# Means of k and v copied side by side and transposed in six full-height blocks, with loads and first folds re-placed

## The chip, the cores and the metric

The kernel runs on one core of one Trainium2 chip. The metric is the device time of one execution in microseconds (us), taken from the chip. Executions of one kernel mostly agree within about half a per cent here, so every comparison rests on several of them, taken in turns with the kernel before on the same chip. Traces have their own clock that starts with the first instruction; the span in a trace is 1 to 3 us shorter than the measured time.

## The reference, cut to what matters

Eight batches of eight heads, 576 tokens, head size 64, 32 memory slots. Each batch is an attention through the 32 slots, and its output feeds a bilinear feed-forward layer that all batches share:

```python
a   = softmax(phi, axis=2)                      # over the 32 slots
k_m = einsum('bhsm,bhsd->bhmd', a, k)           # means of k: per head 32 x 64
v_m = einsum('bhsm,bhsd->bhmd', a, v)           # means of v
attn = softmax(q @ k_m.T / 8)
x   = (attn @ v_m) laid out as tokens x 512
out = ((x @ w_a) * (x @ w_b)) @ w_out           # 512 -> 1536 -> 512
```

The kernel never forms `attn @ v_m`. It multiplies the means of v into w_a and w_b once per batch (a "fold"), and multiplies the weights of attention by that.

## The kernel before

The work of a batch is cut into named units: `exp` (exponential of phi, on ScalarE), `kv` (sums of k and v, on TensorE), `km` (division, giving the means `kvm`, on VectorE), `kvt` (transposes of the means), `qt` (32x32-block transposes of q, on VectorE), `sc` (scores), `e`, `den`, `nr` (softmax), `v0` to `v2` (folds; `x..` copies them out of PSUM). While TensorE does the big products of batch b (`pa`, `pb`, and the down products `po`), the units of batch b+1, and with a prime those of b+2, are dealt out over its 24 slots in a list. The part that the change replaces:

```python
def kv_transpose():
    kvm = t["kvm"]
    t["kvT"] = mid.tile([P, 6, P], F16, name="kvT")
    pT = banks.tile([P, 6, P], F16, name="pT")
    for g in range(2):
        for dh in range(2):
            for z in range(4):
                nc.tensor.transpose(out=pT[32 * z:32 * z + 32, 2 * g + dh, :],
                                    in_=kvm[:, g, 0, 32 * dh:32 * dh + 32],
                                    identity=ident, tile_position=(0, 32 * z))
    # ... and 8 more for the means of v: 24 transposes of 128 x 32 in all
    nc.vector.tensor_copy(out=t["kvT"], in_=pT)
```

Loads are issued by GpSimd; k, v and q become 16 bits wide on the way. phi and q have two buffers each, k and v share two:

```python
def load(b):
    load_phi(b); load_k(b); load_v(b); load_q(b)
# ...
for b in range(2, B):
    if b + 2 < B:
        load(b + 2)                  # at the start of each period
```

Batches 0 and 1 go through separate, denser lists, because the weights and the first inputs are still arriving. Batch 1's chain is filled up with early down products, the "fillers" ("y4" is four of them). A slot of the first folds is four `pa` or `pb` matmuls, 0.49 us; the prediction calls it a half-step.

The softmax here doesn't subtract the row's maximum and nothing guards it: scores larger than these inputs give would overflow.

## Time and profile before

| | before |
|---|---|
| time, median of 3 | 256.01 us (255.79 to 256.13) |
| TensorE (PE) busy | 242.8 us, 95% of the span |
| VectorE, ScalarE, GpSimd busy | 62%, 61%, 14% |
| DMA | full up to 82 us, then in bursts |
| six blocks of 24 small transposes | 0.55 us of TensorE each |

Matmuls are pipelined and their ends are modelled, so busy time says little about how much TensorE can still give. What counts is when one group starts after the one before it. In the views TensorE is PE (its weight loads PEld), VectorE DVE, ScalarE ACT and GpSimd POOL. The prediction shows the lines and how to read them.

### The profile page before, as it was taken

Reading aid. Unit: us, or ns where it says so; the run is one execution under the profiler, and the core shown is the slowest. Engines: PE = TensorE matmul, PEld = TensorE weight load, DVE = VectorE, ACT = ScalarE, POOL = GpSimd, SP = SyncE. Lnnn points to the kernel's source line nnn. Section 1 sums busy time; section 2 is a strip of 40 time slices with the busy share of each in tenths; the row PEclk is TensorE's granted clock in tenths of the full one; section 3 lists DMA queues with packets and bytes.
Section 4 is the critical chain, followed back from the end, with each engine's and each line's share of the span. In section 5 each row is a group of like instructions: output and inputs, shape, how many; then the busy total and the mean of one; then the engine's idle time right before and its main releaser. Section 6 shows DMA issues by size and latency. Waiting matters only on the chain.

```text
span 254.5 us, 7157 instructions
## 1 busy us (share of the span) xinstructions
PE 242.8 (95%) x2887; PEld 140.1 (55%) x2887; DVE 157.8 (62%) x349; ACT 155.7 (61%) x379; POOL 35.4 (14%) x54
## 2 busy tenths in 40 slices
PE   8789599999999999999999999999999999999993
PEld 3455274456554555556565556655665555666642
DVE  6347686367967856875985568746983567445400
ACT  3147472588479479758855777578856667555421
POOL 8733234300300310310121000000000000000000
PEclk9999999999999999999999999999999999999999
DMA  6999999999999696498359521112112112113233
GB/s 143 195 198 206 216 245 207 253 228 272 250 243 208 144 225 135 135 171 153 86 131 222 128 62 44 44 41 44 41 40 49 43 41 45 41 41 70 58 82 82
DMA packets 26033, 33.49 MB, mean 132 GB/s; under 512 B 1936, under 2 KB 20624, under 8 KB 26000
## 3 DMA queue, kind: packets, MB, share of 16 engines
q0 software_dynamic: 19552, 23.01, 50.0%
q1 hardware_dynamic: 6288, 9.90, 15.5%
q8 instruction: 22, 0.36, 0.5%
q10 hardware_dynamic: 160, 0.13, 0.2%
q14 instruction: 11, 0.09, 0.1%
HBM read 42.47 MB, written 9.44 MB: 204 GB/s over the span
## 4 chain that ended last, share of the span: by engine, by line
PE 80%; DMA 11%; DVE 3%; ACT 2%; issue 2%; POOL 1%; ACTq 0%; DVEq 0%; POOLq 0%
PE po L383 34%; PE pa L469 18%; PE pb L479 16%; DMA wb_sb<-in_moe_w_b_dram 6%; PE pva L330 5%; DMA kv_sb<-in_v_dram 4%; PE pkv L206 2%; PE pD L310 1%; PE pscore L288 1%; DVE qT L197 1%; DVE ht L482 1%; PE pk L253 1%; PE pT L232 1%; ACT a_sb L472 1%; POOL q_sb L89 1%
## 5 line engine op out<-in xcount | busy, mean ns | idle before, releaser
L482 DVE TENSOR_TENSOR ht<-a_sb,pb 128x288 f16<-128x288 f16 x192 | 84.1, 447 | 59.2 <-ACT a_sb L472 51.7
L383 PE MATMUL po<-wo_sb,ht 128*128 128x512 f16 x420 | 118.7, 379 | 0.0
L472 ACT CAST a_sb<-pa 128x288 f16<-128x288 f32 x192 | 75.4, 404 | 42.3 <-PE pa L469 36.9
L469 PE MATMUL pa<-A,vab 128*128 128x288 f16 x384 | 76.7, 287 | 0.9 <-DVE A L320 0.7
L479 PE MATMUL pb<-A,vab 128*128 128x288 f16 x384 | 76.1, 286 | 0.2
L469 PEld LDWEIGHTS <-vab 128*128 128x128 f16 x384 | 34.1, 98 | 40.0 <-issue 8.2
L383 PEld LDWEIGHTS <-ht 128*128 128x128 f16 x420 | 40.3, 98 | 19.2 <-issue 0.9
L479 PEld LDWEIGHTS <-vab 128*128 128x128 f16 x384 | 37.1, 98 | 11.7 <-ACT vab L342 1.1
L342 ACT CAST vab<-pva 128x512 f16<-128x512 f32 (+1 forms) x52 | 28.8, 557 | 14.9 <-PE pva L330 14.8
L342 DVE CAST vab<-pva 128x512 f16<-128x512 f32 (+1 forms) x52 | 33.4, 645 | 6.1 <-PE pva L330 5.6
L388 ACT ACTIVATE o_sb<-po 128x512 f32<-128x512 f32 x35 | 21.1, 602 | 11.0 <-PE po L383 9.9
L197 DVE STREAM_TRANSPOSE qT<-q_sb 128x576 f16<-128x576 f16 x32 | 24.2, 764 | 0.0
L301 ACT ACTIVATE E<-pscore 128x288 f16<-128x288 f32 x32 | 11.5, 419 | 13.1 <-PE pscore L288 13.1
L311 ACT ACTIVATE L<-pD 128x288 f32<-128x288 f32 x32 | 11.4, 409 | 8.3 <-PE pD L310 7.9
L145 PE MATMUL pw<-warm 128*128 128x256 f16 (+1 forms) x59 | 11.5, 340 | 1.3 <-DVE warm L114 1.3
L77 POOL DMA_DIRECT2D phi_sb<-in_phi_dram x7 | 5.3, 756 | 52.7 <-ACT a_sb L472 27.2
L188 ACT ACTIVATE exp_sb<-phi_sb 128x576 f16<-128x576 f32 x16 | 11.0, 698 | 2.5 <-DMA phi_sb<-in_phi_dram 2.5
L330 PEld LDWEIGHTS <-kvT 64*32 64x32 f16 x416 | 4.5, 89 | 14.1 <-issue 11.6
L320 DVE TENSOR_TENSOR A<-E,R 128x576 f16<-128x576 f16 (+1 forms) x17 | 7.5, 441 | 7.2 <-ACT R L319 6.2
L330 PE MATMUL pva<-wb_sb,kvT 64*32 64x512 f16 (+1 forms) x208 | 10.1, 362 | 1.9 <-DMA wb_sb<-in_moe_w_b_dram 1.9
L319 ACT ACTIVATE R<-L 128x576 f16<-128x576 f32 (+1 forms) x17 | 11.1, 664 | 0.1
L330 PE MATMUL pva<-wa_sb,kvT 64*32 64x512 f16 (+1 forms) x208 | 10.3, 370 | 0.7 <-DMA wa_sb<-in_moe_w_a_dram 0.7
(43 smaller groups left out, 107.2 us busy)
## 6 DMA issues: line engine op xcount, KB each, us to landing
out_dram<-o_sb SPq DMA_DIRECT2D x70, 128.0 KB, 2.4
kv_sb<-in_v_dram POOLq DMA_DIRECT2D x7, 576.0 KB, 10.5
phi_sb<-in_phi_dram POOLq DMA_DIRECT2D x7, 576.0 KB, 9.8
kv_sb<-in_k_dram POOLq DMA_DIRECT2D x7, 576.0 KB, 10.6
q_sb<-in_q_dram POOLq DMA_DIRECT2D x6, 576.0 KB, 11.2
wo_sb<-in_moe_w_out_dram POOLq DMA_DIRECT2D x3, 512.0 KB, 16.6
q_sb<-in_q_dram POOLq DMA_DIRECT2D x4, 288.0 KB, 12.8
wa_sb<-in_moe_w_a_dram POOLq DMA_DIRECT2D x2, 512.0 KB, 15.1
```

What stands on the lines that cost most here:

```text
L145: nc.tensor.matmul(pw[:, :cols], warm[:, :P], warm[:, :cols], start=True, stop=True)
L197: nc.vector.transpose(out=t["qT"][:, hp, :], in_=qs[b][:, hp, :])
L301: nc.scalar.activation(out=Ev[:, g, :, z, :], in_=pss, func=AF.Exp, scale=1.0 / (8.0 * CS))
L311: nc.scalar.activation(out=t["L", g][:, sl], in_=pD, func=AF.Ln)
L330: nc.tensor.matmul(t["pva", lo, z][g][0][32 * j:32 * j + 32, 0:hi - lo], t["kvT"][64 * r:64 * r + 64, 4 + g, M * j:M * j + M], w_sbs[z][64 ...
L342: engine_copy(out=vabs[b][z][:, g, lo:hi], in_=pva[:, 0:hi - lo])
L383: nc.tensor.matmul(po, hts[pair][:, i, P * c:P * (c + 1)], wo_sb[:, i, :], start=(i == 0), stop=(i == NFF - 1))
L388: nc.scalar.mul(out=o_sb, in_=po, mul=1.0 / (CS * CS))
L469: nc.tensor.matmul(pa, vab[0][:, g, fs], A[:, g, HALF * hf:HALF * (hf + 1)], start=(g == 0), stop=(g == 1))
L472: nc.scalar.copy(out=a_sb, in_=pa)
L479: nc.tensor.matmul(pb, vab[1][:, g, fs], A[:, g, HALF * hf:HALF * (hf + 1)], start=(g == 0), stop=(g == 1))
L482: nc.vector.tensor_tensor(out=ht[:, i, t0:t0 + HALF], in0=a_sbs[hf - hfs[0]], in1=pb, op=ALU.mult)
```

## The change

Its intent: TensorE is the bound, and 24 small transposes in another tiling mode (128*32 in the views, against 128*128) cost it more than six full-height ones. So GpSimd, which has little to do, first copies the means so that each block of 128 columns lies side by side, in the repeated order in which the small transposes placed it. Because GpSimd also issues the loads, those get places of their own ("L"). And the first folds, which had waited for weights, move later, with some filler re-ordered. Shortened:

```diff
+        def repeat():
+            t["rep"] = mid.tile([P, 2, 3, P], F16, name="rep")
+            k, v = (t["kvm"][:, :, x].rearrange("p g (e d) -> p g e d", e=2 - x) for x in range(2))
+            for g in range(2):
+                nc.gpsimd.tensor_copy(out=t["rep"][:, g, 0:2].rearrange("p e (z d) -> p e z d", z=4),
+                                      in_=k[:, g].unsqueeze(2).to_broadcast([P, 2, 4, 32]))
+            nc.gpsimd.tensor_copy(out=t["rep"][:, :, 2:3]...,  in_=v...to_broadcast([P, 2, 2, D]))
         def kv_transpose():
-            # 24 transposes of 128 x 32 at tile_position (0, 32 z)
+            for g in range(2):
+                for x in range(3):
+                    nc.tensor.transpose(out=pT[:, (2 * g + x, 4 + g)[x == 2], :], in_=t["rep"][:, g, x], identity=ident)
 ...
-    ups(steps(0, 4, 12), slots(0, "- v2a+x2a - v2b+x2b"))
-    chain(1, "exp0 exp1 y6 ks0 y4 kt0 qt0 qt1 y2 ks1 y4 kt1 s0 e0 qt2 qt3 y8 den0 s1 e1 nr0 y4 den1 nr1 y3 vs0 y1 vs1 y2 vt0 y1 vt1 y1 "
+    ups(steps(0, 4, 12), slots(0, "- - - - v2a+x2a - v2b+x2b"))
+    chain(1, "exp0 exp1 y9 ks0 y3 kt0 qt0 qt1 y1 ks1 y3 kt1 s0 e0 qt2 qt3 y6 den0 y2 s1 e1 nr0 y4 den1 y2 vs0 vs1 y1 vt0 vt1 nr1 y1 "
 ...   # batch 1's ups re-ordered likewise; in the list of batch 2 "... nr0+L exp0' ..." (load of batch 5)
-    every = ("- sc+e0 ... v2+kv'+x2a km'+x2b qt3' - kvt' -")
+    every = ("- sc+e0 ... v2+kv'+x2a km'+x2b rp' qt3' kvt' L")
     for b in range(2, B):
-        if b + 2 < B:
-            load(b + 2)
+        if b == 2:
+            load(4)
```

More of the change, by code (lines that the diff above doesn't have):

```diff
@@ L223, in take_kv @@
                 banks.free(bank)
+        def repeat():
[4 more added lines that the diff above has]
+                                      in_=k[:, g].unsqueeze(2).to_broadcast([P, 2, 4, 32]))
+            nc.gpsimd.tensor_copy(out=t["rep"][:, :, 2:3].rearrange("p g e (z d) -> p (g e) z d", z=2),
+                                  in_=v.rearrange("p g e d -> p (g e) d").unsqueeze(2).to_broadcast([P, 2, 2, D]))
         def kv_transpose():
-            kvm = t["kvm"]
             t["kvT"] = mid.tile([P, 6, P], F16, name="kvT")
@@ L229, in kv_transpose @@
             for g in range(2):
-                for dh in range(2):
-                    for z in range(4):
-                        nc.tensor.transpose(out=pT[32 * z:32 * z + 32, 2 * g + dh, :],
-                                            in_=kvm[:, g, 0, 32 * dh:32 * dh + 32],
-                                            identity=ident, tile_position=(0, 32 * z))
-            for g in range(2):
-                for z in range(4):
-                    nc.tensor.transpose(out=pT[32 * z:32 * z + 32, 4 + g, :],
-                                        in_=kvm[:, g, 1, 32 * (z % 2):32 * (z % 2) + 32],
-                                        identity=ident, tile_position=(0, 32 * z))
+                for x in range(3):
+                    nc.tensor.transpose(out=pT[:, (2 * g + x, 4 + g)[x == 2], :], in_=t["rep"][:, g, x], identity=ident)
             nc.vector.tensor_copy(out=t["kvT"], in_=pT)
@@ L372, in units @@
         u["km"] = one(take_kv)
+        u["rp"] = one(repeat)
         u["kvt"] = one(kv_transpose)
@@ L519, in unit @@
                 return lambda: work.pull(-work.done % NFF)
+            if n == "L":
+                return lambda: load(b + 2) if b + 2 < B else None
             if n[0] == "y":
@@ L549 @@
     load(2)
-    ups(steps(0, 4, 12), slots(0, "- v2a+x2a - v2b+x2b"))
-    chain(1, "exp0 exp1 y6 ks0 y4 kt0 qt0 qt1 y2 ks1 y4 kt1 s0 e0 qt2 qt3 y8 den0 s1 e1 nr0 y4 den1 nr1 y3 vs0 y1 vs1 y2 vt0 y1 vt1 y1 "
+    ups(steps(0, 4, 12), slots(0, "- - - - v2a+x2a - v2b+x2b"))
+    chain(1, "exp0 exp1 y9 ks0 y3 kt0 qt0 qt1 y1 ks1 y3 kt1 s0 e0 qt2 qt3 y6 den0 y2 s1 e1 nr0 y4 den1 y2 vs0 vs1 y1 vt0 vt1 nr1 y1 "
              "hv0a hx0a y2 hv0b hx0b y2")
     load(3)
-    ups(steps(1, 0, 4), slots(1, "- hv1a+hx1a hv1b+hx1b - v1a+x1a v1b+x1b y2 y2"))
+    ups(steps(1, 0, 4), slots(1, "y1 hv1a+hx1a hv1b+hx1b y1 v1a+x1a v1b+x1b y3 y3"))
     work.plan(S + HALF, 8)
     work.rate = 0
-    ups(half_steps(1, 0, 4), slots(1, "v2a+x2a v2b+x2b exp0'+y2 exp1'+y2 qt0' qt1'+y2 kv'+km' y2+qt2'"))
+    ups(half_steps(1, 0, 4), slots(1, "v2a+x2a+v2b+x2b y9 - exp0' exp1'+qt0' kv'+km' rp'+qt1' qt2'"))
     work.plan(S + HALF, 10)
-    ups(half_steps(1, 1, 4), slots(2, "qt3 kvt - sc+e0 e1 den0 v0+x0a den1+x0b nr0 nr1 v1+x1a x1b"))
-    second = ("v2_+x2a_ exp0+x2b_ exp1+qt0 kv+km qt1 kvt+qt2 qt3 - sc+e0 e1 v0+x0a x0b+den0 den1 v1+x1a x1b+nr0 exp0' nr1 exp1'+qt0' v2+x2a x2b "
-              "kv' km'+qt1' kvt'+qt2' qt3'")
-    every = ("- sc+e0 - e1 v0+x0a x0b den0 den1 exp0' qt0' v1+x1a x1b exp1' nr0 qt1' nr1 qt2' v2+kv'+x2a km'+x2b qt3' - kvt' -")
+    ups(half_steps(1, 1, 4), slots(2, "kvt qt3 - sc+e0 e1 den0 den1 v0+x0a nr0+x0b nr1 v1+x1a x1b"))
+    second = ("v2_+x2a_ exp0+x2b_ exp1+qt0 kv+km rp+qt1 qt2 kvt+qt3 - sc+e0 e1 v0+x0a x0b+den0 den1 v1+x1a x1b+nr0+L exp0' nr1 exp1'+qt0' v2+x2a x2b "
+              "kv'+km' rp'+qt1' qt2' kvt'+qt3'")
+    every = ("- sc+e0 - e1 v0+x0a x0b den0 den1 exp0' qt0' v1+x1a x1b exp1' nr0 qt1' nr1 qt2' v2+kv'+x2a km'+x2b rp' qt3' kvt' L")
     last = "- sc+e0 - e1 v0+x0a x0b den0 den1 - - v1+x1a x1b - nr0 - nr1 - v2+x2a x2b - - - - -"
     for b in range(2, B):
-        if b + 2 < B:
-            load(b + 2)
+        if b == 2:
+            load(4)
         names = second if b == 2 else every if b + 2 < B else last
```

## The prediction

> **What bounds the kernel now.** I read the page first, then busy time in windows of 6 us, then TensorE's timeline where a window is not full, then the timelines of GpSimd and VectorE for what feeds it. The page's first lines, and three windows (start:end, length, then busy us of each engine with its instructions, clock, DMA share, GB/s):
>
> ```profile
> PE 242.8 (95%) x2887; PEld 140.1 (55%) x2887; DVE 157.8 (62%) x349; ACT 155.7 (61%) x379; POOL 35.4 (14%) x54
> DMA  6999999999999696498359521112112112113233
> ...
> 30.00:36.00 6.00, 4.41 (x42) 3.37 (x43) 3.89 (x10) 3.35 (x10) 1.79 (x3) 1.00 1.18 256
> 36.00:42.00 6.00, 6.00 (x105) 3.44 (x106) 3.65 (x10) 2.67 (x7) 1.92 (x3) 1.00 1.23 207
> 186.00:192.00 6.00, 6.00 (x61) 3.75 (x60) 5.04 (x13) 3.28 (x9) 0.00 (x0) 1.00 0.21 46
> ```
>
> TensorE is full from about 32 us to 247 us; no other engine passes 62%. Up to 82 us the DMA is full too, so in that stage landings set when work may start. Busy ends are modelled, so the reader should use starts. In the steady stage two po matmuls start 0.216 us apart and two pa matmuls 0.1225 us apart (4 in 0.49 us): this is an engine limited by what it streams. Only three things can shorten the run: less TensorE time, fewer TensorE waits, or an earlier end of the DMA-bound start. The wait in the start is here (TensorE's timeline: start us, length, group, and the idle before it):
>
> ```profile
> 28.43 0.41 PE L330 MATMUL pva<-wa_sb,kvT 64*32 64x512 f16 x8 [0.71 <-DMA wa_sb<-in_moe_w_a_dram]
> 28.77 0.66 PE L469 MATMUL pa<-A,vab 128*128 128x288 f16 x4
> 29.27 0.65 PE L479 MATMUL pb<-A,vab 128*128 128x288 f16 x4
> 31.59 0.41 PE L330 MATMUL pva<-wb_sb,kvT 64*32 64x512 f16 x8 [1.67 <-DMA wb_sb<-in_moe_w_b_dram]
> ```
>
> Both folds of the last third of the weights wait for their weights. The block of small transposes in the steady stage, timeline and then the groups by line:
>
> ```profile
> 188.52 0.59 PE L383 MATMUL po<-wo_sb,ht 128*128 128x512 f16 x2
> 189.04 0.41 PE L232 MATMUL pT<-ident,kvm 128*32 128x128 f16 x16
> 189.28 0.29 PE L237 MATMUL pT<-ident,kvm 128*32 128x128 f16 x8
> 189.50 0.42 PE L469 MATMUL pa<-A,vab 128*128 128x288 f16 x2
> ...
> L232 PE MATMUL pT<-ident,kvm 128*32 128x128 f16 x96 | 2.6, 222 | 0.1
> L237 PE MATMUL pT<-ident,kvm 128*32 128x128 f16 x48 | 1.7, 219 | 0.0
> ```
>
> The second po started at 188.52 + 0.216 = 188.74, so the next full-height matmul could have started at 188.95; it starts at 189.50. **The block costs 0.55 us**, of which the 24 transposes stream for about 0.35 us (16 of them in 0.24 us), and the rest is the gap on each side.
>
> **What the Trainium skill says.** "TensorEngine Tiling (Array Packing)", Key Properties: a change of tiling mode drains TensorE. The trace agrees: 188.95 to 189.04 is a gap with no wait named, and the same shows around the other packed groups. "TensorE: Matmul & The Clock Gate", Back-to-back issue gap: a 128-column matmul takes 55.6 ns alone in a stream and about 81 ns when each has its own weight load. The trace has no full-height 128-column stream; its 256-column one (pl, 12 in 1.32 us) runs at 110 ns. "GPSIMD Engine Reference", section 3.1: 1.03 to 1.8 cycles per element at 1.2 GHz for one-input work, plus dispatch. No copy by GpSimd is in this trace; its 128-element memset takes 0.25 us and its 128-element selects 0.29 to 0.35 us.
>
> **The change, part by part.**
> 1. *Transposes.* Six batches (2 to 7) use this block. Six full-height ones cost 6 x 0.056 = 0.33 to 6 x 0.081 = 0.49 us; I take 0.40, with no change of mode around them. Gain 0.15 us x 6 = **0.9 us**, all on the path, as TensorE is full.
> 2. *Copies.* Three of 256 elements: 256 x 1.03/1.2 = 0.22 us to 256 x 1.8/1.2 = 0.38 us, plus about 0.2 us of overhead judged from the memset: 0.4 to 0.6 us each, 1.2 to 1.8 us for the three, on an engine with nothing else at that time. They lie between the means (kvm, VectorE) and the transposes. For batch 7 the sums start at 184.39, the last kvm ends at 187.16 + 0.35 = 187.51, and the transposes start at 189.04. The schedule keeps the transposes in the same slot, so 1.5 us are free for 1.2 to 1.8 us of copies: a TensorE wait of 0 to 0.3 us in each of batches 5, 6, 7. I charge **0.3 us** in all. Batches 3 and 4 get one more slot (0.9 to 1.1 us) and are safe, and batch 4 loses the wait it has now (the first transposes at 107.85, the second half at 108.22, 0.26 us "<-DVE kvm"). Batch 2 has about 1.8 us of TensorE work between sums and transposes and now waits some 0.6 us for VectorE there; the means now come before a q transpose, but the copies are added: I call it even. Together **0.3 us** gained.
> 3. *First folds moved three half-steps later (0.49 us each).* The second waits for weights that land at 31.55 whatever TensorE does, so three half-steps are done before it and batch 1's chain starts 1.5 us earlier, at about 36.4. But landings stay. The second half of batch 1's q lands at 26.16 + 17.2 = 43.4; two q transposes (0.72 us each) follow, so its second scores can't start before about 45.05; they start at 45.88 now. Of 1.5 us, **0.8 us** stays.
> 4. *Re-ordering in batch 1's chain.* The two v sums become neighbours, as do the two v transposes, and the two folds of the last third: three pairs of mode changes fewer, about 0.2 us each (a packed group of 4 transposes takes 50.32 to 50.49 where its streaming is 0.06): **0.6 us**. The first filler that needs the last part of w_out (lands 48.8) moves behind the v transposes, so an earlier chain doesn't hit that.
> 5. *Loads.* Now GpSimd's queue holds nothing but loads, and they run ahead of the program until a buffer frees:
>
> ```profile
> 103.25 0.76 POOL L77 DMA_DIRECT2D phi_sb<-in_phi_dram  x1 [12.85 <-ACT a_sb L472]
> 106.33 0.74 POOL L81 DMA_DIRECT2D kv_sb<-in_k_dram  x1 [2.32 <-PE pa L469]
> 111.66 0.74 POOL L89 DMA_DIRECT2D q_sb<-in_q_dram  x1 [3.85 <-DVE qT L197]
> ...
> 149.08 0.77 DVE L197 STREAM_TRANSPOSE qT<-q_sb 128x576 f16<-128x576 f16 x1
> 176.82 0.77 DVE L197 STREAM_TRANSPOSE qT<-q_sb 128x576 f16<-128x576 f16 x1
> ```
>
> Those are batch 6's loads, the first of them 46 us before its q is first used at 149.08. With copies in the same in-order queue, a load waits for every copy ahead of it. Batch 5's load stays ahead of batch 4's copies ("L" in the middle of the period of batch 2). But batch 6's comes after batch 5's copies, about 128.96 + 4.6 = 133.6, and batch 7's after batch 6's, about 157.97 + 4.6 = 162.6. From the issue of phi to the landing of q a set takes 15.5 us (batch 5's: 83.87 to 89.66 + 9.7 = 99.4, the DMA busy throughout). So q lands at about 149.1 and 178.1, against uses at 149.08 and 176.82: **no slack for batch 6, and VectorE late by about 1.3 us for batch 7**. VectorE is 60 to 80% busy there and a few PSUM banks of lead cushion TensorE, so I charge **0.9 us** for both.
>
> Sum: 0.9 + 0.3 - 0.3 + 0.8 + 0.6 - 0.9 = 1.4 us gained, 256.0 - 1.4 = 254.6.
>
> **Rivals.** (a) *The copies become the wait.* If a GpSimd copy takes 0.8 us or more (its two-element-axis broadcast reads are untried here, and VectorE shares its port to SBUF), three take 2.4 us and the transposes wait about 1 us in three to five batches: +3 to +5 us on my sum, 257 to 259. For it: a slack of only 1.5 us. Against: GpSimd's small operations take 0.3 us. (b) *The loads come just too late.* If the queue runs slower than 15.5 us a set, each us is a us of VectorE twice, phi too: +2 to +3 us, about 257. Against: in that stage output traffic is only 45 GB/s. (c) *The start is DMA-bound, so part 3 gives nothing*: then 255.4. For it: DMA full up to 82 us. Against: by 50 us the loads run ahead of their use (batch 2's v lands at 56.0, its sums start at 64.06), so TensorE's work then counts again. (d) *All parts pay and no load is late*, with 0.08 us less per transpose block and all 1.5 us of the start kept: about 252.5. For it: the landings in the start may shift with the issue times.
>
> **Range and chances.** The gains add up to 2.6 us with little doubt about their sign; the two losses are uncertain and one-sided. That gives 254.6, and 8 in 10 for 252.5 to 257.2. Two per cent is 5.1 us: faster than 250.9 needs twice the gains and no loss; slower than 261.1 needs both (a) and (b) at their worst.
>
> **What would show it.** Transposes: six full-height matmuls with starts of 56 to 81 ns apart and no gap around them; wrong if a wait on POOL stands before them. Copies: three POOL groups of 0.4 to 0.6 us. Start: the fold at 31.6 again, with less idle before it, and batch 1's second scores near 45.1. Loads: batch 7's phi issue near 160 to 163, and a VectorE wait for q before its first q transpose; wrong if there is none, or if TensorE idles over 1 us after it. The prediction fails if windows after 84 us show TensorE clearly below full.

## The result, and the profile after

The changed kernel takes **254.04 us** (median of 4 runs, 253.52 to 254.41) against 255.9 us for the kernel before (4 runs). The ratio is 0.9926, with a 95% interval of 0.9905 to 0.9947. A ratio here is the mean time of one kernel's fast runs over that of the other's of the same rounds, so it is not quite the ratio of the medians. At a limit of 2% this counts as the same time, but the gain of 1.9 us is clear of the noise. The prediction was 254.6 us, with 252.5 to 257.2 as its range.

The busy times on the page of the changed kernel:

```profile
PE 241.7 (96%) x2779; PEld 141.0 (56%) x2779; DVE 157.5 (62%) x349; ACT 156.0 (62%) x379; POOL 42.1 (17%) x72
```

Two of its windows of 6 us, in the columns of the prediction's first fence:

```profile
30.00:36.00 6.00, 5.11 (x48) 3.71 (x46) 4.71 (x12) 3.91 (x11) 1.86 (x3) 1.00 1.18 256
...
174.00:180.00 6.00, 4.93 (x46) 2.91 (x46) 4.39 (x11) 4.24 (x10) 0.00 (x0) 1.00 0.18 39
```

The window from 30 us got 0.7 us fuller, and one that used to be full, from 174 us (6.00 us busy before), has a hole of 1.07 us. TensorE's timeline at the first folds:

```profile
29.25 0.41 PE L332 MATMUL pva<-wa_sb,kvT 64*32 64x512 f16 x8
29.59 0.67 PE L482 MATMUL pb<-A,vab 128*128 128x288 f16 x4
30.09 0.65 PE L472 MATMUL pa<-A,vab 128*128 128x288 f16 x4
31.64 0.41 PE L332 MATMUL pva<-wb_sb,kvT 64*32 64x512 f16 x8 [0.89 <-DMA wb_sb<-in_moe_w_b_dram]
```

The fold of w_b starts where it did, with the weights' landing, but more is done before it. The new transposes in the same timeline:

```profile
186.87 0.59 PE L386 MATMUL po<-wo_sb,ht 128*128 128x512 f16 x2
187.31 0.50 PE L241 MATMUL pT<-ident,rep 128*128 128x128 f16 x6
187.64 0.41 PE L472 MATMUL pa<-A,vab 128*128 128x288 f16 x2
```

The copies on GpSimd (POOL), as a group of the page (busy us, mean ns):

```profile
L230 POOL COPY rep<-kvm 128x256 f16<-128x256 f16 x12 | 4.8, 402 | 115.8 <-DVE rphi L220 71.5
```

The second po starts at 186.87 + 0.216 = 187.09 and its stream is over at 187.30. The transposes start at 187.31 and the next matmul 0.33 us later, with no gap on either side. A block costs 0.33 us, where it was 0.55 (five of the six; batch 2's takes 0.49 us). A copy takes 0.40 us. Now GpSimd's queue, and what waits for it, from the timelines of the three engines:

```profile
130.13 0.40 POOL L232 COPY rep<-kvm 128x256 f16<-128x256 f16 x1
130.48 0.75 POOL L77 DMA_DIRECT2D phi_sb<-in_phi_dram  x1
...
158.92 0.40 POOL L232 COPY rep<-kvm 128x256 f16<-128x256 f16 x1
159.27 0.76 POOL L77 DMA_DIRECT2D phi_sb<-in_phi_dram  x1
...
161.47 0.78 POOL L89 DMA_DIRECT2D q_sb<-in_q_dram  x1
...
175.03 0.59 PE L386 MATMUL po<-wo_sb,ht 128*128 128x512 f16 x2
...
175.52 0.78 DVE L197 STREAM_TRANSPOSE qT<-q_sb 128x576 f16<-128x576 f16 x1 [1.48 <-DMA q_sb<-in_q_dram]
...
176.69 0.40 PE L472 MATMUL pa<-A,vab 128*128 128x288 f16 x2 [1.07 <-DVE ht L485]
```

Batch 6's loads start at 130.5 us, where the kernel before had them at 103 us; batch 7's at 159.3, before at 124.6. They stand directly behind a copy. Batch 7's q lands 16.2 us after that (issued at 161.47, 14.0 us to landing), VectorE waits 1.48 us for it, and TensorE then waits 1.07 us for VectorE. So loads that the source places ahead reach the DMA *later* than before.

Where the time went, by the starts of the score groups in the two traces:

| start of | before | after | difference |
|---|---|---|---|
| batch 1's chain (first po) | 37.83 | 36.40 | -1.43 |
| batch 1's second scores | 45.88 | 44.88 | -1.00 |
| batch 2's scores | 70.28 | 68.85 | -1.43 |
| batch 3's scores | 90.28 | 88.33 | -1.95 |
| batch 4's scores | 111.43 | 109.00 | -2.43 |
| batch 5's scores | 138.29 | 135.63 | -2.66 |
| batch 6's scores | 166.86 | 163.99 | -2.87 |
| batch 7's scores | 193.72 | 191.85 | -1.87 |
| last products | 247.44 | 245.57 | -1.87 |

The gain comes in steps of 0.2 to 0.5 us per batch after a start that gives 1.4 us, and 1.0 us of it is lost in the one period in which batch 7's q is late.

### The profile page after: what moved, and what is told of

The parts are those of the page before. It is cut to its first block, busy times and chain, and to the rows that moved or that the text cites. A ratio compares the mean times of both kernels' runs of the same rounds, so it can differ in the third digit from the quotient of the medians.

```text
span 252.6 us, 6966 instructions
## 1 busy us (share of the span) xinstructions
PE 241.7 (96%) x2779; PEld 141.0 (56%) x2779; DVE 157.5 (62%) x349; ACT 156.0 (62%) x379; POOL 42.1 (17%) x72
## 4 chain that ended last, share of the span: by engine, by line
PE 75%; DMA 16%; POOL 2%; DVE 2%; ACT 1%; issue 1%; ACTq 0%; DVEq 0%; POOLq 0%
PE po L386 32%; PE pa L472 16%; PE pb L482 15%; DMA wb_sb<-in_moe_w_b_dram 6%; DMA q_sb<-in_q_dram 6%; PE pva L332 4%; DMA kv_sb<-in_v_dram 4%; PE pkv L206 2%; PE pD L312 1%; PE pscore L290 1%; PE pT L241 1%; POOL kv_sb L81 1%; POOL q_sb L89 1%; DVE qT L197 1%; PE pl L412 1%
## 5 line engine op out<-in xcount | busy, mean ns | idle before, releaser
L230 POOL COPY rep<-kvm 128x256 f16<-128x256 f16 x12 | 4.8, 402 | 115.8 <-DVE rphi L220 71.5
L145 PE MATMUL pw<-warm 128*128 128x256 f16 (+1 forms) x59 | 12.5, 360 | 1.3 <-DVE warm L114 1.3
```

Source lines behind the costliest of these rows:

```text
L145: nc.tensor.matmul(pw[:, :cols], warm[:, :P], warm[:, :cols], start=True, stop=True)
```

## The experiments

My theory after this: the start and the transposes gain about 3 us, and batch 7's late q takes 1 us back. The rivals: the late q costs nothing in the end; the transposes' gain is paid for by waits on the copies; the start is bound by landings, so what is gained there is fixed by DMA. Twelve runs of ten kernels, all correct. "Ratio" is always to the kernel before.

**after_again**, the changed kernel itself, as a base.

> The changed kernel once more, as the base for the others on this chip: 254.0 us, ratio to before 0.993. Its trace should again show VectorE waiting about 1.5 us for batch 7's q and TensorE idle about 1.1 us right after it (172 to 178 us).

Measured: 254.57 us, ratio 0.9941 (0.9915 to 0.9966). Its trace has the same waits, smaller: VectorE waits 0.94 us for batch 7's q and TensorE 0.52 us after it. So the size of this wait varies from execution to execution, as landings do.

**loads_first**: the loads move in front of the copies of their period.

```diff
-    every = ("- sc+e0 ... rp' qt3' kvt' L")
+    every = ("L sc+e0 ... rp' qt3' kvt' -")
```

> Only the loads of batches 6 and 7 move: from the end of the period (behind the copies in GpSimd's queue) to its first slot (ahead of them). My theory (the late q of batch 7 cost TensorE about 1.1 us): 252.9 us, 1.1 us below the changed kernel, no VectorE wait for q after 84 us, and TensorE windows from 84 to 240 us all full. Rival (the late load costs nothing in the end, since VectorE catches up, or the earlier traffic costs as much elsewhere): 254.0 us, as the changed kernel.

Measured: 253.57 us, ratio 0.9907 (0.9884 to 0.9930); run again (below) 252.87 us, 0.9901 (0.9882 to 0.9919). In the first the means are 253.49 and 254.45 us, 0.96 us apart. GpSimd's queue in the second run, loads_first_b:

```profile
105.39 0.40 POOL L232 COPY rep<-kvm 128x256 f16<-128x256 f16 x1
105.74 0.75 POOL L77 DMA_DIRECT2D phi_sb<-in_phi_dram  x1
```

And its window where the changed kernel has the hole:

```profile
174.00:180.00 6.00, 6.00 (x53) 3.63 (x38) 5.58 (x13) 5.45 (x12) 0.00 (x0) 1.00 0.19 41
```

Batch 6's loads leave at 105.7 instead of 130.5 us, and the window that had the hole is full. From batch 6's to batch 7's scores it takes 26.62 us; the changed kernel took 27.86 (27.32 in after_again), the kernel before 26.86. In time, the two intervals overlap (0.9884 to 0.9930 here, 0.9915 to 0.9966 for after_again), but all six executions of loads_first (252.93 to 253.70 us) lie below all six of after_again (253.84 to 254.93 us), and VectorE no longer waits for q after 84 us. The theory holds; the rival falls.

**loads_first_old_transposes**: loads_first with `repeat` empty and the 24 small transposes of before.

> As loads_first, but with the 24 small transposes of before and no copies. Theory (a block costs 0.55 us with small transposes and 0.34 us with full-height ones, on the path): 6 x 0.21 = 1.3 us above loads_first, so about 254.2 us. Rival (the block's gap is absorbed elsewhere, or the copies cost as much in waits as the block gains): equal to loads_first within 0.4 us.

Measured: 254.03 us, ratio 0.9930 (0.9908 to 0.9953), 0.5 us above loads_first with overlapping intervals, though all six executions (253.81 to 254.56 us) lie above all six of loads_first. The traces are clearer. From batch 2's scores to the last products, five blocks of transposes lie in between: 245.25 - 68.66 = 176.59 us here, 244.88 - 69.39 = 175.49 us in loads_first. That is 1.10 us, or 0.22 us a block. The pair once more:

> loads_first_old_transposes again, because its first timing (0.6 us above loads_first, intervals overlapping) doesn't tell 0 from the 1.1 us that its trace shows from batch 2's scores to the end (0.22 us a block). Theory: 0.5 to 1.2 us above loads_first_b. Rival (nothing): equal.

> loads_first again, beside the next two on one chip: ratio to before 0.991, 253.6 us.

Measured: loads_first_old_transposes_b 254.06 us, ratio 0.9943 (0.9928 to 0.9959); loads_first_b 252.87 us, 0.9901 (0.9882 to 0.9919). Now the intervals are apart: 0.42% of 255.6 us is 1.1 us. The transposes' gain, net of what the copies cost, is real, and for batches 3 to 7 all of it is on the path. For batch 2's block, which takes 0.49 us even with full-height transposes (65.36 to 65.85 us in loads_first_b), the two traces differ by only 0.1 us (from the chain's first po to batch 2's scores 32.97 us with the small transposes, 32.88 us in loads_first_b).

**loads_first_copies_twice**: each batch's three copies made twice.

```diff
-            for g in range(2): ...copies...
+            for _ in range(2):
+                for g in range(2): ...copies...
```

> As loads_first, with each batch's three copies made twice, so 1.2 us more between the means and the transposes. Theory (the slack after the copies is 0.56 us in batches 5 to 7, 0.8 in batch 4, 1.3 in batch 3, none in batch 2): TensorE waits 0.65 x 3 + 0.4 + 0 + 1.2 = 3.5 us more, about 256.4 us. Rival (copies lie beside other work with room to spare): 253 us, as loads_first.

Measured: 255.81 us, ratio 1.0000 (0.9977 to 1.0023), so 0.93% or 2.4 us above loads_first. The copies are on the edge of the path, as the theory says, but the step was smaller than the 3.5 us that I reckoned. TensorE's timeline for batch 5:

```profile
132.25 0.28 PE L242 MATMUL pT<-ident,rep 128*128 128x128 f16 x2
132.79 0.40 PE L242 MATMUL pT<-ident,rep 128*128 128x128 f16 x4 [0.27 <-POOL rep L233]
```

Two of the six transposes start before the last copy is done; only the rest waits. Between score groups this kernel takes 0.43 to 0.45 us longer than loads_first_b in the periods that hold the transposes of batches 5, 6 and 7 (I had 0.65), 0.22 for batch 4, nothing for batch 3, and 1.07 for batch 2.

**old_fold_place**: only the first folds back where they were.

```diff
-    ups(steps(0, 4, 12), slots(0, "- - - - v2a+x2a - v2b+x2b"))
+    ups(steps(0, 4, 12), slots(0, "- v2a+x2a - v2b+x2b"))
```

> The changed kernel with the folds of the last third of the weights back in their old slots. Theory A (of my prediction: landings of q hold batch 1's second scores, so only 0.8 of the 1.5 us stay): batch 1's chain starts 1.4 us later (37.8), its second scores only 0.8 us later (45.7), and the time is 0.8 us above the changed kernel, 254.9. Theory B (from the trace of after: what ate 0.4 us is a wait of the second k transposes for VectorE, which moves along with the chain): second scores 1.4 us later (46.3), time 255.4.

Measured: 255.85 us, ratio 0.9994 (0.9982 to 1.0006). Against 0.9926 and 0.9941 of the changed kernel this is 0.5 to 0.7%, 1.4 to 1.7 us, not 0.8 us. The chain starts at 37.62 and the second scores at 46.10; in the traces this kernel is 1.2 us behind the changed one there (46.10 against 44.88), and still at batch 6's scores (165.20 against 163.99). Theory B is nearer. The wait that it names is the first of these two, in the changed kernel:

```profile
42.21 0.29 PE L273 MATMUL pT<-ident,kvm 128*32 128x128 f16 x8 [0.43 <-DVE kvm L265]
...
43.30 1.44 DVE L197 STREAM_TRANSPOSE qT<-q_sb 128x576 f16<-128x576 f16 x2 [0.45 <-DMA q_sb<-in_q_dram]
```

VectorE does two q transposes before the means of k's second half, and only four fillers, where there were six, lie between on TensorE. In old_fold_place the wait is there too (0.42 us); it moves with the chain. But theory A's landing is there too: every kernel with the folds in the new place has VectorE waiting for the second half of batch 1's q at this point, for 0.45 us (the second line) to 1.01 us, and neither of the two with the old place has. In the changed kernel TensorE's wait for the means came first and hid it. In after_again, where the chain starts 0.40 us earlier (36.00), the second scores start at 44.48 and stretch to 0.87 us, twice their usual length, and the next filler starts at 45.29, against 45.25 in the changed kernel: the landing took those 0.4 us back. So both theories name a real limit, at nearly the same time; what this run refutes is A's size.

**old_chain**: batch 1's chain and its first ups in the old order, the copies put beside a q transpose.

```diff
-    chain(1, "exp0 exp1 y9 ks0 y3 ... den1 y2 vs0 vs1 y1 vt0 vt1 nr1 y1 "
+    chain(1, "exp0 exp1 y6 ks0 y4 ... den1 nr1 y3 vs0 y1 vs1 y2 vt0 y1 vt1 y1 "
 ...  # and the three lists after it as before, with rp' added
```

> The changed kernel with batch 1's chain and its first ups in the old order (folds and loads stay new; the copies go in beside the last q transpose but one). Theory (three pairs of mode changes more, and the filler that needs the last of w_out is early again): from batch 1's second scores to batch 2's scores 0.6 us longer, time 0.6 us above the changed kernel, 254.7 us, and the second k transposes without the 0.43 us wait. Rival (order makes no difference because batch 2's sums are held by exp and loads anyway): 254.1 us.

Measured: 255.40 us, ratio 0.9979 (0.9963 to 0.9996), 0.4 to 0.5% or 1.0 to 1.4 us above the changed kernel, about twice what I expected (its interval just touches that of after_again). From batch 1's second scores to batch 2's scores it takes 25.25 us, 1.28 us more than in the changed kernel. The execution traced, 254.56 us, was the fastest of the six. The 0.43 us wait is gone, but another has come:

```profile
48.48 0.59 PE L386 MATMUL po<-wo_sb,ht 128*128 128x512 f16 x2 [0.58 <-DMA wo_sb<-in_moe_w_out_dram]
```

With the chain earlier, the old order reaches the last part of w_out before it has landed. The prediction named this danger as avoided, without saying what it was worth. Another 0.30 us is a wait of batch 2's transposes for the copies (at 67.38), which this order leaves less room, so the run doesn't measure the mode changes alone. The new order pays in a second way too: batch 2's to batch 3's scores take 19.76 us here and 19.48 us in the changed kernel.

**loads_at_start**: all loads at the start of a period, as in the kernel before.

```diff
-    ... v1+x1a x1b+nr0+L exp0' ...        # and "L" out of `every`
+    ... v1+x1a x1b+nr0 exp0' ...
-        if b == 2:
-            load(4)
+        if b + 2 < B:
+            load(b + 2)
```

> The changed kernel with every load issued at the start of its period, as before, so that batch 5's load too stands behind batch 4's copies in GpSimd's queue. Theory: load of batch 5 at about 106 instead of 85 us, its q lands near 121.5, VectorE wants it near 119: a second VectorE wait of about 2.5 us, TensorE idle about 2 us near 120 us, time about 256 us. Rival (the placing of the loads is of no account): 254.1 us.

Measured: 256.03 us, ratio 1.0000 (0.9987 to 1.0014). In the timeline of all engines:

```profile
105.92 0.40 POOL L232 COPY rep<-kvm 128x256 f16<-128x256 f16 x1
106.59 0.77 POOL L77 DMA_DIRECT2D phi_sb<-in_phi_dram  x1 [0.27 <-issue]
...
121.64 0.78 DVE L197 STREAM_TRANSPOSE qT<-q_sb 128x576 f16<-128x576 f16 x1 [2.54 <-DMA q_sb<-in_q_dram]
...
122.81 0.41 PE L472 MATMUL pa<-A,vab 128*128 128x288 f16 x2 [2.12 <-DVE ht L485]
```

Issue, landing and both waits came where they were expected. Without the new place of batch 5's load, the whole change would have been worth nothing.

**q_second**: the changed kernel, with q loaded right after phi in batches 5 to 7.

```diff
         load_phi(b)
+        if b > 4:
+            load_q(b)
         load_k(b)
         load_v(b)
-        load_q(b)
+        if b <= 4:
+            load_q(b)
```

> The changed kernel, loads placed as there, but in batches 5 to 7 q is loaded right after phi and before k and v. Theory (only q of batch 7 is too late; k and v have 20 us and more): batch 7's q lands about 9 us after the issue of phi instead of 15, no VectorE wait for q after 84 us, time as loads_first, 253.5 us. Rival (loads_first gained by something else, such as quieter DMA queues during the copies): 254.3 us, as the changed kernel.

Measured: 253.32 us, ratio 0.9916 (0.9898 to 0.9934). VectorE starts batch 7's first q transpose at 174.15 us right behind its neighbour, with no wait. The ratio lies between loads_first_b (0.9901) and the changed kernel, and its interval overlaps those of both, so time alone doesn't place it. The trace does: from batch 6's to batch 7's scores it takes 26.64 us, as loads_first_b (26.62). The late q explains the hole: it goes although the loads are still issued late.

**loads_first_exp_earlier** and **loads_first_three_waits** try to win the waits that are left in the start.

```diff
-    ... "v2a+x2a+v2b+x2b y9 - exp0' exp1'+qt0' kv'+km' rp'+qt1' qt2'"
+    ... "v2a+x2a+v2b+x2b y9 exp0' exp1' qt0' kv'+km' rp'+qt1' qt2'"
```

(three_waits adds: `kvt` after `qt3` in the next list, and one filler moved in front of `ks1`.)

> As loads_first, with batch 2's two exponentials one slot earlier, because TensorE waits 0.58 us for the second of them in the middle of batch 2's sums (62.4 to 63.0 us in the trace of after). Theory: that wait goes, 0.4 to 0.6 us below loads_first, 253.0 us. Rival (VectorE's means are then the next wait, so nothing is won): 253.5 us.

> loads_first with three small waits of the start taken on at once: batch 2's exponentials one slot earlier, its transposes one slot later (so that they don't wait for the copies), and one filler moved in front of batch 1's second k sums. If those waits are on the path: up to 0.7 us below loads_first_b, 252.9 us. Rival (a wait of the start is passed on to the next engine): equal to loads_first_b within 0.3 us.

Measured: 253.72 us, ratio 0.9919 (0.9905 to 0.9933), and 253.09 us, 0.9912 (0.9897 to 0.9928, beside loads_first_b at 0.9901). Neither gains. In the first, the wait for the exponential shrinks from 0.58 to 0.28 us, and the transposes of the same batch now wait for the copies:

```profile
66.32 0.40 PE L241 MATMUL pT<-ident,rep 128*128 128x128 f16 x4 [0.44 <-POOL rep L232]
```

In the second the wait of 0.43 us for the means is gone, that for the exponential is 0.28 us again, and the transposes don't wait for the copies. But with the transposes a slot later, batch 2's scores now wait for VectorE's copy of the transposed means:

```profile
68.60 0.50 PE L290 MATMUL pscore<-qT,kvT 32*32 32x288 f16 x32 [0.63 <-DVE kvT L242]
```

With 0.23 us for w_out, that makes 1.14 us of waits between 36 and 70 us, where loads_first_b has 1.01 us (0.43 and 0.58). Batch 2's scores start 0.1 us before those of loads_first_b, and the time is no better within the noise. The waits were passed on, as the rival said.

loads_first is the best version that I ran: 0.9901 and 0.9907 of the kernel before, against 0.9926 and 0.9941 for the change as made.

## Why the prediction was right, and where not

The time and the balance were right: gains of some 3 us at the start and in the transposes, about 1 us lost to late loads, 1.9 us measured against 1.4 forecast. The sizes of the parts were less so, and that they still sum to nearly the right time is partly luck (see the end of this section). By its own steps:

1. *Transposes, 0.9 us.* Right in kind, too small: a block saves 0.21 to 0.22 us and not 0.15, because six full-height transposes take 0.33 us and not 0.40. Five blocks give 1.1 us; the sixth, batch 2's, takes 0.49 us and gives 0.1. loads_first_b and its twin differ by 1.1 us in time.
2. *Copies, 0.3 us charged.* Each takes 0.40 us, the lower end of my 0.4 to 0.6. The first starts while the second half of the means is still being made, so the last one for batch 7 ends at 186.35 + 0.40 = 186.75 against transposes at 187.31: 0.56 us of slack and no wait. The charge was too high by 0.3. Rival (a) falls, but only by this margin: with the copies doubled, loads_first gains nothing over the kernel before. Batch 4's 0.26 us came back as forecast: 0.48 us saved between the scores of batches 3 and 4, less 0.22 for the block. Batch 2, called even, has a wait that I did not see: 0.58 us in its sums, for the exponential.
3. *First folds, 0.8 of 1.5 us.* The size at the second scores was near (1.00 us), and the limit named, **"landings stay"**, is real (old_fold_place above). But "can't start before about 45.05" is a slip: its own terms, 43.4 and two transposes of 0.72 us, give 44.84; and the first of these scores need only the first of the two transposes, so they started at 44.88 and 44.48. What it left out is the wait of 0.43 us for VectorE, which comes from the new filler counts and which in the changed kernel took the shift before the landing could. The worth was mis-sized: taking the shift away cost 1.2 us in the traces and 1.4 to 1.7 us of the whole, not 0.8.
4. *Re-ordering, 0.6 us.* Mis-sized: the old order costs 1.0 to 1.4 us, with 0.58 us of it as a wait for w_out and 0.30 us as one for the copies. What three pairs of mode changes cost alone wasn't measured.
5. *Loads, 0.9 us charged.* Right in mechanism and size: phi of batch 7 forecast for "near 160 to 163", issued at 159.3; the forecast VectorE wait of 1.3 us measured 1.48 us (0.94 in the second); batch 6 came through with no wait; TensorE lost 1.07 us (0.52), and taking the lateness away gave 1.0 us. Two of the signs of being wrong that the prediction set itself came up, though: TensorE idle for over 1 us after the wait (1.07 us in the first trace, not in the second), and a window after 84 us clearly below full (4.93 of 6 us). The second was badly chosen, since the loss that it charged has to show as just such a window. Rival (b), slower landings, hardly showed (16.2 us a set for 15.5), and rival (c), a start that gives nothing, is refuted by old_fold_place. Rival (d), no load late and about 252.5 us, is nearly what loads_first then measured (252.87 and 253.57 us).

The parts that were mis-sized (1 to 4) all erred on the same side. Taken one at a time, the experiments give 1.1 us for transposes with copies, 1.4 to 1.7 for the folds, 1.0 to 1.4 for the order and 1.0 lost to the late q: 2.5 to 3.2 us in all, where 1.9 was measured and 1.4 forecast. The parts don't simply add: in the dense start one wait takes over from another, as in batch 2's sums. The prediction added parts that were too small as if they were independent; the two errors partly cancelled.

## What to carry to other kernels

Before work is given to an idle engine, look at what else stands in that engine's queue: GpSimd was idle, but its empty queue was what let the loads run ahead, and three short copies in it held batch 6's first load back by 27 us and batch 7's by 35 us. A place in the source is not a time; a load behind an instruction that waits for this period's results can't be issued before them, so put it ahead of that instruction, or order its parts by when they are needed. And when a wait is removed in a tightly packed start, measure the whole: the same shift can be held by a landing, be held by another engine, or come through, and a wait that is taken away can come back on the next engine.

## What the Trainium skill lacked or had wrong

- "TensorE: Matmul & The Clock Gate", Back-to-back issue gap: of its two figures for 128 columns, about 56 ns for a matmul alone and about 81 ns in pairs of weight load and matmul, the first is right here even with a weight load each: six transposes in 0.33 to 0.34 us, 55 to 57 ns each, in five of the six blocks. Its Part 4 gives about 275 ns for one transpose in a kernel; one record here lasts 219 ns, but that is not what a block costs, since the next one starts 55 to 57 ns later.
- "TensorEngine Tiling (Array Packing)", Key Properties, names the drain at a mode change but no cost. Here a block of 24 packed transposes cost 0.55 us for some 0.35 us of streaming, so by estimate about 0.2 us for the two changes.
- "TensorE: Matmul & The Clock Gate" calls GpSimd's queue a strict FIFO in its first table, but no page that I read draws the consequence for loads: a load behind a copy waits for what the copy waits for. Here that moved batch 6's loads from 103 to 130 us.
